# Value matmuls grouped by the height of their chunks, and a reordered list of work, in an attention and MoE kernel on one core

## Chip, cores and metric

One core of a Trainium2 chip runs the kernel. The metric is the device time of one launch in microseconds. TensorE is called PE here, its weight loads PEld, VectorE DVE, ScalarE ACT, GpSimd POOL and SyncE SP; SP issues nearly all transfers.

## What is computed

Attention over 4 batches, 8 heads, 576 positions of 64 numbers, with a bias that a small network makes of the relative position, and behind it two dense layers with h - tanh(h) between them, on 2304 tokens:

```python
scores = scale * np.matmul(q, k.transpose(0, 1, 3, 2))
x = (psi_rel / psi_i)[..., None]
bias = np.maximum(x @ w1 + b1, 0.0) @ w2
attn = softmax(scores + bias.transpose(2, 0, 1)[None, :, :, :])
x = np.matmul(attn, v)          # heads side by side: 2304 x 512
h = x @ w_in                    # 512 x 2048
out = (h - np.tanh(h)) @ w_out  # 2048 x 512
```

The inputs are fp32. The kernel splits each operand of the large matmuls into a high and a low half (hi, lo) and sums three or four products of halves.

## The kernel before

The work is written as a list of operations with the tiles that they read and write, an engine or several to choose from, an estimated duration and a priority. `Plan.order` (L158) walks through estimated time and gives each free engine the ready operation with the lowest priority number for which buffers are free. The outcome is a fixed list for each engine; on the chip each engine runs its own list in order and waits where a semaphore is not yet set. So durations in the plan issue nothing, they only set the order; SP's transfers are such a list too. `claimed` (L110) keeps shared buffers for a blocked operation of higher priority.

The operations, by the names that rows and text use:

- **pb** (`bias_group`, L417): 36 groups. Four rows hg are made on ACT, DVE or POOL (L429 to L433), PE multiplies them by w2 (L441), ACT or DVE scale the result (bo) and SP writes it to bias_d in DRAM.
- **ws, win, wout** (`weight_chunk`, L459): 32 chunks of the two weight matrices, 16 of each. A chunk is loaded into a stage buffer and split with six instructions on DVE, ACT or POOL (L469 to L488).
- **kv, qq** (L502, L513): keys with values, and queries, loaded and split.
- **ps, s, mx** (`attn_tile`, L536): scores of 128 queries by 576 keys for two heads on PE (16 matmuls, L555); DVE adds the bias and takes row minima (L569), ACT the exponential (L583), DVE the reciprocal, ACT the high half hl and DVE the low half (L599), SP the transpose of hl to pt (L609). The two PSUM tiles ps have one buffer each, so the next scores or pb wait until DVE has read the last.
- **px, xt** (`attn_values`, L617): the values. For two batches (bb) and a pair of heads (j) PE sums attention times values over 576 keys. A pair of heads has nine stored chunks of 128 rows: four for each head (i from 0 to 3), and one that both share, 64 rows each (i = 4). Each chunk is taken three times (hi by hi, hi by lo, lo by hi), so a px has 2 x 5 x 3 x 2 = 60 matmuls. The matmuls of j = 0 and 1 write to PSUM partitions 0 to 63 and 64 to 127. Before, each batch is a sum of its own, first its four chunks of 128 rows, then the shared one. ACT and DVE turn px into xt (L645, L648).
- **ph, tt, gh, gl, po** (`moe`, L656): the dense layers of a block of 128 or 256 tokens: hidden matmuls ph (L669), tanh on ACT, subtraction on DVE, halves gh and gl, output matmuls po (L696), in steps of 24 or 48.

Names carry their place: px{block}_{pair}; s{g}_{t}_{pair}_{bb}, with g a pair of batches, t a tile of 128 queries and t = 4 the half tile of 64; `BLOCKS` (L39) takes (0, 4) first. In an engine's order the scores' two tiles of s0_1_0_1 are ps0_0_1_0_1 and ps1_0_1_0_1, and a running number stands at the end.

Priorities are steps of the attention tiles plus or minus leads (L765 to L773); the weight chunks have the one line `W_P` for both matrices, taken in turn by fours. `WEIGHT` (L754) scales durations where an operation may choose its engine.

Of the kernel before, what the change touches and what calls it, by code (L numbers as in the profile page):

```python
# [300 lines left out]
def kernel(  # L301
# [157 lines left out]
    def weight_chunk(src, hi, lo, key, prio):  # L459
        st = new_stage(f"ws_{key[0]}{key[1]}_{key[2]}")  # L460
# [5 lines left out]
        move(P * 4096, lambda: st()[:, :1024].bitcast(U64), src, w=[(st, 0), (st, 1)], prio=prio)  # L466
# [69 lines left out]
    def attn_tile(g, t, p, bb, qq, bt, prio):  # L536

        half = t == HALF
        nm = f"{g}_{t}_{p}_{bb}"
# [24 lines left out]
        op("pe", c_mm(HS, 1, 2 * len(terms)), scores, r=rd, w=pss + [(s, "x") for s in rows], prio=prio)  # L564
        for j in range(2):
# [14 lines left out]
            op("dve", c_psum(S) + 80, bias_min, r=[ps, (bt, 0), (bt, 1)], w=[s, (m, j)], prio=prio, psum=True)  # L580
# [6 lines left out]
            op("act", c_act(S, 1) + 190, expo, r=[(m, j)], w=[s, (m, 2 + j)], prio=prio)  # L587
# [5 lines left out]
        op("dve", 331, recip, r=[(m, 2), (m, 3)], w=[(m, 6)], prio=prio)  # L593
        for j in range(2):
# [9 lines left out]
            op(high, r=[s, (m, 6)], w=[(hl, j, 0)], prio=prio)  # L604
            op("dve", c_dve2(S, 1), low, r=[s, (m, 6), (hl, j, 0)], w=[(hl, j, 1)], prio=prio)
# [11 lines left out]
    def attn_values(g, t, p, pts, px, xt, prio):  # L617
# [3 lines left out]
        runs = [(l, y, i) for i in range(5) for l, y in ((0, 0), (0, 1), (1, 0))]  # L621

        def mms():
            for bb in range(2):
                kw, pt, col = kvt[2 * g + bb, p], pts[0 if half else bb], 64 * bb if half else 0
                for si, (l, y, i) in enumerate(runs):
                    for j in range(2):
# [216 lines left out]
```

## Time and profile before

| | |
|---|---|
| median of 3 runs | 704.25 us (704.04 to 706.08) |
| the profiled execution | 701.42 us, of which the span from first to last instruction 699.6 us |
| TensorE's granted clock, mean | 0.945 of full speed |
| busy: PE, DVE, ACT, POOL | 630.5, 478.8, 429.0, 68.1 us |

Busy is the union of an engine's instructions; PE's ends are modelled, so a busy PE is one that always has a matmul under way. Where an engine's list waits, the profile names the instruction that ended the wait. A clock of 1.00 is 2.4 GHz, of 0.50 it is 1.2.

### The profile page before, as it was taken

The numbers are of one execution on the slowest core, as the hardware profiler recorded it, in microseconds if no ns is written. First come the engines' busy times: TensorE is split into PE (matmuls) and PEld (weight loads), VectorE is DVE, ScalarE is ACT, GpSimd is POOL, SyncE is SP. The second block draws the span as 40 slices with busy tenths as digits, with TensorE's granted clock in tenths as the row PEclk, the third lists the DMA queues.
The fourth block names the chain that finished last, engine by engine and source line by source line (L and its number), as shares of the span: only waits on it lengthen the run. The fifth ranks groups of instructions, "written<-read, shape, count | busy, mean of one in ns | idle before, by whom it ended". The sixth has DMA issues, their size and how long they took to land.

```text
span 699.6 us, 18910 instructions
## 1 busy us (share of the span) xinstructions
PE 630.5 (90%) x8096; PEld 488.0 (70%) x8096; DVE 478.8 (68%) x980; ACT 429.0 (61%) x788; POOL 68.1 (10%) x61
## 2 busy tenths in 40 slices
PE   4556566796999999999999999999999999999997
PEld 1112234684677777788888878887887888888897
DVE  5998998889866667585888867665776746532231
ACT  5768876658776767567666676666665646422221
POOL 1100111101210301100221010021000000000000
PEclk9768857899899999999999999999999999999999
DMA  7877799988775866666979876777769666630000
GB/s 251 286 275 247 235 236 309 229 180 172 191 174 96 210 151 152 110 161 139 259 200 212 187 179 137 155 149 165 152 147 154 123 124 129 119 54 31 2 31 17
DMA packets 193780, 114.25 MB, mean 163 GB/s; under 512 B 171152, under 2 KB 176416, under 8 KB 193696
## 3 DMA queue, kind: packets, MB, share of 16 engines
q1 hardware_dynamic: 193632, 113.03, 68.4%
q8 instruction: 63, 1.03, 0.6%
q14 instruction: 21, 0.17, 0.1%
q0 software_dynamic: 64, 0.02, 0.0%
HBM read 55.22 MB, written 15.34 MB: 101 GB/s over the span
## 4 chain that ended last, share of the span: by engine, by line
PE 78%; DVE 4%; ACT 1%; issue 1%; DVEq 0%; ACTq 0%
PE ph L669 28%; PE po L696 27%; PE px L630 10%; PE ps L555 10%; PE pb L441 3%; DVE s L569 1%; DVE hl L599 1%; DVE hg L431 0%; ACT hl L370 0%; DVE tt L686 0%; DVE gl L389 0%; ACT hg L429 0%; DVE win_lo L389 0%; ACT tt L681 0%; DVE bo L451 0%
## 5 line engine op out<-in xcount | busy, mean ns | idle before, releaser
L669 PE MATMUL ph<-xt,win_hi 128*128 128x256 f16 (+1 forms) x1280 | 194.5, 263 | 0.1
L669 PE MATMUL ph<-xt,win_lo 128*128 128x256 f16 (+1 forms) x640 | 162.1, 263 | 0.0
L696 PE MATMUL po<-gh,wout_h 128*128 128x256 bf16 (+1 forms) x640 | 161.9, 263 | 0.0
L696 PE MATMUL po<-gl,wout_h 128*128 128x256 f16 (+1 forms) x640 | 161.4, 262 | 0.1
L696 PE MATMUL po<-gh,wout_l 128*128 128x256 bf16 (+1 forms) x640 | 161.4, 262 | 0.0
L583 ACT ACTIVATE s<-s,mx 128x576 f32<-128x576 f32 x144 | 110.6, 769 | 55.3 <-DVE mx L569 49.1
L669 PEld LDWEIGHTS <-win_hi 128*128 128x128 f16 x1280 | 117.2, 98 | 23.0 <-issue 11.7
L696 PEld LDWEIGHTS <-wout_h 128*128 128x128 f16 x1280 | 116.5, 98 | 19.4 <-issue 7.8
L599 DVE SCALAR_TENSOR_TENSOR hl<-s,mx,hl 128x576 f16<-128x576 f32 x144 | 117.5, 847 | 9.9 <-ACT hl L370 9.6
L569 DVE CUSTOM_DVE_ANT_0 s<-ps,bt 128x576 f32<-128x576 f32 x144 | 104.7, 751 | 26.5 <-PE ps L555 26.3
L441 PE MATMUL pb<-hg,w2s 128*32 128x288 f32 x576 | 74.9, 496 | 46.1 <-ACT hg L429 19.3
L370 ACT ACTIVATE hl<-s,mx 128x576 f16<-128x576 f32 x144 | 104.3, 765 | 9.6 <-issue 6.1
L686 DVE SCALAR_TENSOR_TENSOR tt<-tt,ph 128x512 f32<-128x512 f32 x72 | 49.4, 686 | 83.3 <-ACT tt L681 83.0
L555 PE MATMUL ps<-kv,qq 64*128 64x288 f16 (+1 forms) x1280 | 90.3, 298 | 16.5 <-DVE mx L569 10.2
L681 ACT ACTIVATE tt<-ph 128x512 f32<-128x512 f32 x72 | 43.0, 597 | 99.4 <-PE ph L669 99.0
L630 PE MATMUL px<-pt,kv 128*64 128x128 f16 (+3 forms) x2400 | 85.4, 221 | 2.5 <-DMA pt<-hl 2.5
L555 PEld LDWEIGHTS <-qq 64*128 64x128 f16 (+1 forms) x1280 | 55.8, 101 | 44.8 <-issue 31.2
L441 PEld LDWEIGHTS pb<-hg,w2s 128*32 128x32 f32 x576 | 24.7, 123 | 87.3 <-ACT hg L429 40.7
L630 PEld LDWEIGHTS <-kv 128*64 128x64 f16 (+1 forms) x2400 | 69.6, 113 | 21.3 <-issue 10.6
L669 PEld LDWEIGHTS <-win_lo 128*128 128x128 f16 x640 | 62.9, 98 | 5.9
L696 PEld LDWEIGHTS <-wout_l 128*128 128x128 f16 x640 | 62.6, 98 | 6.1 <-issue 0.2
L429 ACT ACTIVATE hg<-zt,b1l 128x576 f32<-128x576 f32 x86 | 61.8, 766 | 0.0
(52 smaller groups left out, 467.5 us busy)
## 6 DMA issues: line engine op xcount, KB each, us to landing
bt<-bias_d SPq DMA_DIRECT2D x32, 576.0 KB, 4.6
bias_d<-bo SPq DMA_DIRECT2D x36, 288.0 KB, 3.6
kvst<-kv SPq DMA_DIRECT2D x16, 576.0 KB, 5.6
ws_wi<-w_in SPq DMA_DIRECT2D x16, 512.0 KB, 5.3
ws_wo<-w_out SPq DMA_DIRECT2D x16, 512.0 KB, 4.8
bt<-bias_d SPq DMA_DIRECT2D x16, 288.0 KB, 5.3
qst<-qF SPq DMA_DIRECT2D x8, 512.0 KB, 4.0
outT<-ot SPq DMA_DIRECT2D x16, 256.0 KB, 2.5
```

The source lines that it names most:

```text
L370: "act": ("act", c_act(n, ptr), lambda: A.activation(out(), in_(), AF.Copy, scale=scale() if ptr else scale)),
L429: lambda hg=hg, src=src, bs=bs: A.activation(hg(), src, AF.Relu, bias=bs, scale=1.0)),
L441: nc.tensor.matmul(pb()[32 * j : 32 * j + 32, x, :HS], w2s, hgs[j]()[:, x * HS : x * HS + HS], start=True, stop=True, tile_position=(0, 32 ...
L555: nc.tensor.matmul(pss[j]()[w * e : w * e + w, x, :HS], qq()[dp, a, c0 + w * e : c0 + w * e + w], ks()[dp, y, x * HS : x * HS + HS], start ...
L569: V.tensor_tensor_reduce(s().rearrange("p (x k) -> p x k", x=2), ps()[:, :, :HS], bt()[:, j].rearrange("p (x k) -> p x k", x=2), -0.125 / ...
L583: A.activation(s(), s(), AF.Exp, bias=m()[:, j : j + 1], scale=-1.0, accum_out=m()[:, 2 + j : 3 + j])
L599: V.scalar_tensor_tensor(hl()[:, 1, hs], s(), m()[:, 6 + j : 7 + j], hl()[:, 0, hs], ALU.mult, ALU.subtract)
L630: nc.tensor.matmul(px()[64 * j : 64 * j + 64, w * bb : w * bb + w], kw()[r, y, S + 64 * c : S + 64 * c + 64], pt()[r, NCH * l + c, col : c ...
L669: nc.tensor.matmul(ph()[:, n * (f - f0) : n * (f - f0) + n], w[:, k, f * P : f * P + P], xs[k]()[:, a, :n], start=(k == 0 and e == 0), sto ...
L681: "act", c_actp(512), lambda ph=ph, tt=tt: A.activation(tt(), ph(), AF.Tanh, scale=1.0 / SH),
L686: lambda ph=ph, tt=tt: V.scalar_tensor_tensor(tt(), tt(), -SH, ph(), ALU.mult, ALU.add),
L696: nc.tensor.matmul(po()[:, d // 2, n * (d % 2) : n * (d % 2) + n], wout[w][:, f, d * P : d * P + P], x()[:, n * (f - f0) : n * (f - f0) + ...
```

## The change

Two things. First, `attn_values` runs all chunks of 128 rows of both batches and then the shared chunks of both, with one start flag on the first matmul and one stop flag on the last. The number and shape of the matmuls are the same.

Second, the list of work. The planner's durations of scores and values are larger; weight chunks have a line of priorities for each matrix and their loads a later one (`W_LEAD`); a table `ADJ` adds to the priorities of single operations; ACT counts for less where an engine is chosen; some leads differ; `claimed` goes through the ready operations in order of priority. `DRAIN` is 0, so the five priorities with it stay.

```diff
@@ claimed
-        for o in {o for ops in cand.values() for o in ops if o.ready <= now}:
-            new = [b for b in o.bufs if not b.live]
-            if new and not self.fits(o, free, limit) and self.fits(o, free, limit, False):
-                for b in new:
-                    if b.tag in self.mixed:
-                        g = self.group[b.tag]
-                        claims[g] = min(claims.get(g, (9e9, 0)), (o.prio, o.idx))
+        ready = {o for ops in cand.values() for o in ops if o.ready <= now}
+        for o in sorted(ready, key=lambda o: (o.prio, o.idx)):
+            groups = {self.group[b.tag] for b in o.bufs if not b.live and b.tag in self.mixed}
+            if groups <= claims.keys():
+                continue
+            if not self.fits(o, free, limit) and self.fits(o, free, limit, False):
+                for g in groups:
+                    claims.setdefault(g, (o.prio, o.idx))
@@ bias_group, and likewise weight_chunk, prep_kv, prep_q, load_bias, attn_tile
+        prio += adj(f"b{t}")
@@ weight_chunk
-        move(P * 4096, lambda: st()[:, :1024].bitcast(U64), src, w=[(st, 0), (st, 1)], prio=prio)
+        move(P * 4096, lambda: st()[:, :1024].bitcast(U64), src, w=[(st, 0), (st, 1)], prio=prio - W_LEAD)
@@ attn_tile
-        op("pe", c_mm(HS, 1, 2 * len(terms)), scores, r=rd, w=pss + [(s, "x") for s in rows], prio=prio)
+        op("pe", c_mm(HS, 1, 2 * len(terms)) + 190.0, scores, r=rd, w=pss + [(s, "x") for s in rows], prio=prio)
@@ attn_values
-        runs = [(l, y, i) for i in range(5) for l, y in ((0, 0), (0, 1), (1, 0))]
+        runs = [(bb, i) for bb in range(2) for i in range(4)] + [(0, 4), (1, 4)]
 
         def mms():
-            for bb in range(2):
+            for n, (bb, i) in enumerate(runs):
                 kw, pt, col = kvt[2 * g + bb, p], pts[0 if half else bb], 64 * bb if half else 0
-                for si, (l, y, i) in enumerate(runs):
+                for m, (l, y) in enumerate(((0, 0), (0, 1), (1, 0))):
...
-                            start=(si == 0),
-                            stop=(si == len(runs) - 1),
+                            start=(n == 0 and m == 0),
+                            stop=(n == 9 and m == 2),
...
-        op("pe", 2 * len(runs) * max(c_mm(w), 53.0), mms, r=rd, w=[px, (xt, "x")], prio=prio)
+        op("pe", 3 * len(runs) * max(c_mm(w), 53.0) + 280.0, mms, r=rd, w=[px, (xt, "x")], prio=prio)
@@ the list of weight chunks
-                    win_chunk(k, c, W_P[0] + W_P[1] * (8 * c + k))
+                    win_chunk(k, c, WI_P[0] + WI_P[1] * (4 * c + k))
                 for f in range(4):
-                    wout_chunk(4 * c + f, W_P[0] + W_P[1] * (8 * c + 4 + f))
+                    wout_chunk(4 * c + f, WO_P[0] + WO_P[1] * (4 * c + f))
@@ numbers
-WEIGHT = {"swdge": 0.8, "dve": 1.125, "act": 0.931, "pool": 0.768}
+WEIGHT = {"swdge": 0.8, "dve": 1.125, "act": 0.803, "pool": 0.768}
...
-W_P = (-15.256, 0.924)
+WI_P = (-15.256, 1.848)
+WO_P = (-11.56, 1.848)
+W_LEAD = -2.426
+DRAIN = 0.0
...
```

What it moves shows in the engines' lists. In the lists of PE below one row stands for each operation, its first matmul. The first place is PE's list at the start of attention, in the half block, where scores of four pairs and the first values stand. Before:

```order
L555 MATMUL ps0_0_4_1_0_652<-kv0_1_94,qq0_4_554 64x288
...
L441 MATMUL pb11_701<-hg44_574,w2s_75 32x288
...
L555 MATMUL ps0_0_4_2_0_737<-kv0_2_144,qq0_4_554 64x288
...
L441 MATMUL pb12_798<-hg48_772,w2s_75 32x288
...
L555 MATMUL ps0_0_4_3_0_812<-kv0_3_175,qq0_4_554 64x288
...
L630 MATMUL px0_0_858<-pt0_4_0_0_726,kv0_0_88 64x64
...
L630 MATMUL px0_1_944<-pt0_4_1_0_793,kv0_1_94 64x64
```

After the change:

```order
L565 MATMUL ps0_0_4_1_0_583<-kv0_1_94,qq0_4_487 64x288
...
L446 MATMUL pb9_644<-hg36_503,w2s_75 32x288
...
L565 MATMUL ps0_0_4_2_0_666<-kv0_2_144,qq0_4_487 64x288
...
L641 MATMUL px0_0_723<-pt0_4_0_0_641,kv0_0_88 64x64
...
L446 MATMUL pb10_790<-hg40_656,w2s_75 32x288
...
L565 MATMUL ps0_0_4_3_0_816<-kv0_3_174,qq0_4_487 64x288
...
L641 MATMUL px0_1_872<-pt0_4_1_0_711,kv0_1_94 64x64
```

The first values now stand ahead of the last scores of the half block, and two bias groups fewer stand ahead of them.

The second place is PE's list in block 2, from the scores of pair 0, second batch (s0_1_0_1), to those of pair 1, second batch (s0_1_1_1). Before:

```order
L555 MATMUL ps0_0_1_0_1_2201<-kv1_0_91,qq0_1_852 128x288
...
L630 MATMUL px1_3_2233<-pt0_0_3_0_2113,kv0_3_175 64x128
...
L441 MATMUL pb19_2304<-hg76_2220,w2s_75 32x288
...
L669 MATMUL ph1_0_2322<-xt0_0_0_1644,win_hi_71 128x256
...
L555 MATMUL ps0_0_1_1_0_2361<-kv0_1_94,qq0_1_852 128x288
...
L696 MATMUL po0_1498<-gh0_12_1950,wout_h_78 128x128
...
L441 MATMUL pb20_2445<-hg80_2348,w2s_75 32x288
...
L669 MATMUL ph1_2_2458<-xt0_0_0_1644,win_hi_71 128x256
...
L555 MATMUL ps0_0_1_1_1_2499<-kv1_1_97,qq0_1_852 128x288
```

After the change:

```order
L565 MATMUL ps0_0_1_0_1_2136<-kv1_0_91,qq0_1_1030 128x288
...
L680 MATMUL ph0_12_2160<-xt0_4_0_803,win_hi_71 128x128
...
L446 MATMUL pb19_2223<-hg76_2154,w2s_75 32x288
...
L641 MATMUL px1_3_2244<-pt0_0_3_0_1932,kv0_3_174 64x128
...
L680 MATMUL ph1_0_2329<-xt0_0_0_1566,win_hi_71 128x256
...
L565 MATMUL ps0_0_1_1_0_2362<-kv0_1_94,qq0_1_1030 128x288
...
L680 MATMUL ph1_2_2384<-xt0_0_0_1566,win_hi_71 128x256
...
L446 MATMUL pb20_2421<-hg80_2307,w2s_75 32x288
...
L565 MATMUL ps0_0_1_1_1_2441<-kv1_1_97,qq0_1_1030 128x288
```

48 hidden matmuls of block 0 (ph0_12) have come behind the first scores, px1_3 behind pb19, and 48 output matmuls (po0) have left this stretch; they now stand right behind its end.

The third place is DVE's list between the minima of pairs 2 and 3 of the half block (ISA rows are the minima and their read). Before:

```order
L469 TENSOR_SCALAR ws_wo9_0_649<-ws_wo9_0_649 128x512
L469 TENSOR_SCALAR ws_wo10_0_693<-ws_wo10_0_693 128x512
L474 SCALAR_TENSOR_TENSOR ws_wo9_0_649<-ws_wo9_0_649 128x512
L590 TENSOR_SCALAR mx0_4_2_0_778<-mx0_4_2_0_778 128x2
L591 RECIPROCAL mx0_4_2_0_778<-mx0_4_2_0_778 128x2
L373 TENSOR_SCALAR ws_wo9_0_649<-ws_wo9_0_649 128x512
L474 SCALAR_TENSOR_TENSOR ws_wo10_0_693<-ws_wo10_0_693 128x512
L482 SCALAR_TENSOR_TENSOR ws_wo9_0_649<-ws_wo9_0_649 128x512
L373 TENSOR_SCALAR ws_wo10_0_693<-ws_wo10_0_693 128x512
L482 SCALAR_TENSOR_TENSOR ws_wo10_0_693<-ws_wo10_0_693 128x512
L389 TENSOR_TENSOR wout_l_79<-ws_wo9_0_649,wout_h_78 128x512
L569 ISA s0_4_3_0_0_855,mx0_4_3_0_856<-ps0_0_4_3_0_812,bt0_4_3_710 128x576
```

After the change:

```order
L579 ISA s0_4_2_0_0_786,mx0_4_2_0_787<-ps0_0_4_2_0_666,bt0_4_2_617 128x576
L579 ISA mx0_4_2_0_787 128x1
L488 SCALAR_TENSOR_TENSOR ws_wo8_0_577<-ws_wo8_0_577 128x512
L579 ISA s0_4_2_0_1_800,mx0_4_2_0_787<-ps1_0_4_2_0_668,bt0_4_2_617 128x576
L579 ISA mx0_4_2_0_787 128x1
L659 SCALAR_TENSOR_TENSOR xt0_4_0_803<-px0_0_723,xt0_4_0_803 128x128
L475 TENSOR_SCALAR ws_wi2_2_637<-ws_wi2_2_637 128x512
L436 TENSOR_SCALAR hg44_850<-zt_80,b1l_76 128x576
L600 TENSOR_SCALAR mx0_4_2_0_787<-mx0_4_2_0_787 128x2
L601 RECIPROCAL mx0_4_2_0_787<-mx0_4_2_0_787 128x2
L480 SCALAR_TENSOR_TENSOR ws_wi2_2_637<-ws_wi2_2_637 128x512
L579 ISA s0_4_3_0_0_863,mx0_4_3_0_864<-ps0_0_4_3_0_816,bt0_4_3_702 128x576
```

Weight chunks have left this stretch, and the low half of the first values (xt0_4_0, which waits for px0_0) has come into it, ahead of the minimum of pair 3.

## Rows read from the trace of the kernel before

**Rows 1.** The page, part 2: PE's busy tenths in 40 slices of 17.5 us
```profile
PE   4556566796999999999999999999999999999997
```

**Rows 2.** By stretch: us; busy us of PE, PEld, DVE, ACT, POOL; clock; DMA share, GB/s
```profile
20.00:176.00 156.00, 104.43 (x1338) 60.47 (x1338) 141.26 (x283) 114.79 (x198) 17.92 (x16) 0.78 0.88 240
176.00:183.00 7.00, 5.78 (x54) 3.26 (x56) 6.54 (x14) 5.78 (x10) 1.04 (x2) 0.51 0.76 211
183.00:630.00 447.00, 447.00 (x5829) 360.30 (x5826) 300.99 (x643) 280.28 (x540) 44.68 (x36) 1.00 0.72 154
sum 700.00, PE 630.47 PEld 488.01 DVE 478.77 ACT 429.02 POOL 68.06; mean PE 126.09 PEld 97.60 DVE 95.75 ACT 85.80 POOL 13.61
```

**Rows 3.** Waits of PE, whole span: us in total, times, longest us
```profile
PE pb L441 <- ACT hg L429: 19.3, 12, 3.8
PE ps L555 <- DVE mx L569: 10.2, 6, 4.2
PE px L630 <- DMA pt<-hl: 2.5, 1, 2.5
```

**Rows 4.** PE's timeline and chain around its last wait: start us, us
```profile
179.35 2.10 PE L555 MATMUL ps<-kv,qq 64*128 64x288 f16 x16 [0.83 <-ACT bo L450]
181.38 2.93 PE L630 MATMUL px<-pt,kv 128*64 128x128 f16 x60
...
189.24 2.79 PE po L696 x48
```

**Rows 5.** PE's timeline in narrow windows through one group px
```profile
303.05 0.86 PE L630 MATMUL px<-pt,kv 128*64 128x128 f16 x24
303.84 0.24 PE L630 MATMUL px<-pt,kv 64*64 64x128 f16 x2
304.13 0.25 PE L630 MATMUL px<-pt,kv 128*64 128x128 f16 x2
304.92 0.35 PE L630 MATMUL px<-pt,kv 64*64 64x128 f16 x6
305.21 1.15 PE L555 MATMUL ps<-kv,qq 64*128 64x288 f16 x16
```

**Rows 6.** The chain that ended last: start us, us, line and count
```profile
195.85 1.09 PE ps L555 x16
...
199.67 2.15 PE px L630 x60
201.82 1.11 PE pb L441 x16
202.93 2.73 PE ph L669 x24
...
623.60 4.25 PE px L630 x180
```

**Rows 7.** Groups of DVE instructions, shapes apart: busy us, mean ns of one
```profile
L389 DVE TENSOR_TENSOR gl<-tt,gh 128x512 f16<-128x512 f32 x50 | 35.0, 701 | 14.7 <-ACT gh L370 14.6
L431 DVE TENSOR_SCALAR hg<-zt,b1l 128x576 f32<-128x576 f32 x58 | 30.6, 556 | 0.3 <-POOL b1l L415 0.3
L389 DVE TENSOR_TENSOR win_lo<-ws_wi,win_hi 128x512 f16<-128x512 f32 x14 | 9.6, 685 | 0.2 <-ACT win_hi L370 0.2
L451 DVE TENSOR_SCALAR bo<-pb,rls 128x576 f32<-128x576 f32 x11 | 9.0, 817 | 9.5 <-PE pb L441 9.3
L389 DVE TENSOR_TENSOR qq<-qst,qq 128x1024 f16<-128x1024 f32 x3 | 4.2, 1395 | 0.0
L373 DVE TENSOR_SCALAR win_hi<-ws_wi 128x512 f16<-128x512 f32 x5 | 2.1, 420 | 0.0
```

**Rows 8.** The tile pt: its transposes
```profile
DMA to landing us min/median/max: 4.5/5.0/10.1
```

**Rows 9.** Timelines of PE and SP: the first scores, the first transpose
```profile
82.41 0.69 PE L555 MATMUL ps<-kv,qq 64*64 64x288 f16 x16 [1.04 <-ACT bo L450]
92.22 5.40 SPq L609 DMA_TRANSPOSE pt<-hl  x1
```

More of the change, by code (lines that the diff above doesn't have):

```diff
@@ L415, with adj @@
     op("pool", c_pool(144, 1), lambda: G.tensor_scalar(b1l, b1l, b1s, 1.0, ALU.mult, ALU.mult), r=["b1"], w=["b1l"], prio=-1000)
+    def adj(name):
+        return ADJ.get(name, 0.0)
     def bias_group(t, prio):
+        prio += adj(f"b{t}")
         hgs = [new_hg(f"hg{4 * t + j}") for j in range(4)]
@@ L459, in weight_chunk @@
     def weight_chunk(src, hi, lo, key, prio):
+        prio += adj("%s%d%d" % key)
         st = new_stage(f"ws_{key[0]}{key[1]}_{key[2]}")
@@ L502, in prep_kv @@
     def prep_kv(b, p, prio):
+        prio += adj(f"kv{b}{p}")
         kw, st = new_kv(f"kv{b}_{p}"), new_stage(f"kvst{b}_{p}")
@@ L513, in prep_q @@
     def prep_q(g, t, prio):
+        prio += adj(f"q{g}{t}")
         n = 512 if t == HALF else 1024
@@ L524, in load_bias @@
     def load_bias(g, t, p, prio):
+        prio += adj(f"bt{g}{t}{p}")
         bt = new_bt(f"bt{g}_{t}_{p}")
@@ L538, in attn_tile @@
         half = t == HALF
+        prio += adj(f"u{g}{t}{p}{bb}")
         nm = f"{g}_{t}_{p}_{bb}"
@@ L578, in bias_min @@
                 )
-            op("dve", c_psum(S) + 80, bias_min, r=[ps, (bt, 0), (bt, 1)], w=[s, (m, j)], prio=prio, psum=True)
+            op("dve", c_psum(S) + 80, bias_min, r=[ps, (bt, 0), (bt, 1)], w=[s, (m, j)], prio=prio - DRAIN, psum=True)
             def expo(s=s, j=j):
@@ L585, in expo @@
                 )
-            op("act", c_act(S, 1) + 190, expo, r=[(m, j)], w=[s, (m, 2 + j)], prio=prio)
+            op("act", c_act(S, 1) + 190, expo, r=[(m, j)], w=[s, (m, 2 + j)], prio=prio - 2 * DRAIN)
         def recip():
@@ L591, in recip @@
             V.reciprocal(m()[:, 6:8], m()[:, 4:6])
-        op("dve", 331, recip, r=[(m, 2), (m, 3)], w=[(m, 6)], prio=prio)
+        op("dve", 331, recip, r=[(m, 2), (m, 3)], w=[(m, 6)], prio=prio - 3 * DRAIN)
         for j in range(2):
@@ L603, in attn_tile @@
             high = narrow(S, lambda hs=hs: hl()[:, 0, hs], s, lambda j=j: m()[:, 6 + j : 7 + j], 1, kind="hi")
-            op(high, r=[s, (m, 6)], w=[(hl, j, 0)], prio=prio)
-            op("dve", c_dve2(S, 1), low, r=[s, (m, 6), (hl, j, 0)], w=[(hl, j, 1)], prio=prio)
+            op(high, r=[s, (m, 6)], w=[(hl, j, 0)], prio=prio - 3 * DRAIN)
+            op("dve", c_dve2(S, 1), low, r=[s, (m, 6), (hl, j, 0)], w=[(hl, j, 1)], prio=prio - 3 * DRAIN)
         pt = new_pt(f"pt{nm}")
@@ L766 @@
 TR_LEAD = 654.549
-KV0_LEAD = 55.926
-KV_LEAD = 1.3
-Q_LEAD = 97.336
+KV0_LEAD = 51.88
+KV_LEAD = 3.864
+Q_LEAD = 137.041
 Q0_LEAD = -2.194
@@ L772 @@
 BIAS_P = (-20, 1.684)
-W_P = (-15.256, 0.924)
+WI_P = (-15.256, 1.848)
+WO_P = (-11.56, 1.848)
+W_LEAD = -2.426
+DRAIN = 0.0
+ADJ = {"wo60": 0.437, "wo00": -0.35, "wo130": 0.423, "wi21": 0.211, "wi33": 0.41, "wi00": -0.347, "wo110": 2.613, "wo80": -1.771, "kv31": 1.833, "kv23": 0.652, "kv32": 3.471, "kv12": -1.698, "q11": -8.554, "q10": 1.355, "q12": -0.365, "q14": 0.264, "wo140": -1.074, "b31": -2.52, "kv21": -6.337, "kv13": 9.655, "u1321": -0.833, "u1231": 0.062, "b22": 0.708, "bt141": -0.039, "b15": -0.872, "bt030": -8.756}
 def _tables():
```

## The prediction

> **What bounds the kernel now.** I read first the page's slices of PE's busy time: four to seven tenths in the first eight and in the tenth, nine or more from the eleventh (175 us on) to the last but one [rows 1]. The table by stretch says what the other engines do there [rows 2]: from 183 to 630 us PE is busy for 447.00 of 447.00 us at the full clock, DVE for 301 and ACT for 280. From 20 to 176 us it is the other way round: DVE is busy for 141 of 156 us and PE for 104. The list of waits says whom PE waits for: among others the rows hg of a bias group, 19.3 us by ACT's, and DVE's row minima, which free the scores' PSUM, 10.2 us; for a transposed tile it waits once, 2.5 us [rows 3]. The last wait before the tail is 0.83 us ahead of the scores at 179.35 us [rows 4]. So there are two stages. Up to about 180 us the instructions of DVE set the pace; from there on the end is that moment plus the work left on PE. The last 70 us, with 4 us of waits behind the last hidden and output matmuls, hold no values and keep their order.
>
> **The value matmuls.** A group px has 60 matmuls in 30 pairs; the two of a pair go to the two column halves of the array. In the kernel before, a group runs 12 pairs over chunks of 128 keys, 3 pairs on the shared chunk of 64, and the same again for the second batch. The timeline of one group [rows 5] shows what each turn costs: the first long run starts at 303.05, the short one at 303.84, the next long one at 304.13, the short one at 304.92, and the scores behind it at 305.21. Twelve pairs and a turn take 0.79 us, three pairs and a turn 0.29 (303.84 to 304.13). The difference, 0.50 us for 9 pairs, is 0.0556 us a pair. A whole group takes 2.15 us on the chain [rows 6]; 30 pairs are 1.67 of it, so the four turns are 0.48, 0.12 each. After the change a group has 24 long pairs, then 6 short ones: two turns fewer, **0.24 us**, 11% of a group. The number of matmuls stays 60.
>
> The Trainium skill ("TensorEngine Tiling (Array Packing)", Key Properties) says that a change of tiling mode drains the engine, and the trace agrees that a turn costs, by 0.12 us. "TensorE: Matmul & The Clock Gate" (Step-by-step) gives some 128 cycles for a drain; an estimate by it alone, 128 cycles at 2.4 GHz, would be 0.05 us a turn and 3.4 us for the whole gain; no row here shows a turn that cheap, and I go by the measured 0.12.
>
> How many of them count? Of the 40 groups, px0_0 to px1_2 run ahead of the last wait, where PE stands still anyway: nothing. px1_3 runs at 181.38 us [rows 4], on the border of the two stages; I leave it out. The 32 groups of px2 to px9 run in the stretch in which PE never stops: 32 x 0.24 = **7.7 us**. For the four groups of px9 (64 columns, three of them in 4.25 us [rows 6]) the price of a turn is taken over from the wide ones; at nothing for these four the sum is 6.7. Turns between operations don't change it: counted in the two orders, PE goes from one kind of operation to another (hidden and output matmuls as one kind) 212 times in both.
>
> **The order of the start.** The lists differ most here. DVE's list ahead of the first minimum of pair 0 of the half block (s0_4_0) has 103 rows in place of 121; ahead of s0_1_0_1 296 in place of 307; ahead of s0_1_1_0 318 in place of 321. So attention is pulled ahead of weight chunks, which come later, and by s0_1_1_0 both lists have done nearly the same. I price that last place by kinds [rows 7]: on L373 six more win_hi and one more wout_h, four fewer ws_wi and two fewer ws_wo, all of one shape, net one at 0.42; two more qq of 1024 columns (1.395); one win_lo less (0.685) and one ws_wo of L482 less, taken at the same price; five hg fewer (0.556); one bo more (0.817): 0.42 + 2.79 - 0.69 - 0.69 - 2.78 + 0.82 = **-0.1 us**. And PE, in its list, has by then done the same set of operations in both kernels (the second place in the lists above). If DVE keeps its pace, this place comes at the same time, and behind it lies 7.7 us less work: the sum is **-7.8 us**.
>
> One place further the picture is less kind. In the order before, 48 output matmuls of block 0 (po0, 2.79 us at 189.24 [rows 4]) stand between s0_1_1_0 and s0_1_1_1; now they come behind it. If DVE still bounds there, the gain is 7.7 - 2.8 + 0.1 = 5.0 us. But in the trace PE no longer waits there, and DVE does not fill its time (from 183 us on it is busy for 67%), so I take this as the low end only. One place earlier it is kinder: ahead of s0_1_0_1 DVE has 11 instructions fewer, at its mean of 478.77 us / 980 = 0.49 us some 5.4 us [rows 2], while 48 hidden matmuls (ph0_12, 2.79 us as the same shape elsewhere takes [rows 4]) are pushed behind it. If nothing waits after that, the gain is 7.7 + 5.4 - 2.8 = 10.3 us.
>
> **What costs nothing by this reading.** Other choices of engine: 11 of the subtractions gl go from POOL to DVE, 11 x 0.701 = 7.7 us [rows 7]; they lie nearly all behind 183 us, where DVE has 146 us to spare [rows 2]; without that cover they would eat the gain. Matmul costs in the planner (190 and 280 ns more), DRAIN (0) and the claims of buffers issue nothing; they act through the order alone. Scores and values stand closer in PE's list: summed with the durations of [rows 6], 17.5 us of work at the least lay between a pair's last scores and its px, and 31 in the mean (px2 to px8); now it is 15.9 and 24, and 1.1 for the scores themselves. A transpose needs 4.5 to 10.1 us to land [rows 8], and the chain ahead of it some 10 (scores at 82.41, transpose issued at 92.22 [rows 9]). So 14.5 to 20 us are needed and 17 are there: at most 3 us each, at the two or three closest places; I take zero, since the median landing is 5.0.
>
> **The rivals.**
> *The start gains too.* The place that decides moves to s0_1_0_1 as worked out: -10.3; and the slow stretch of 176 to 183 us (clock 0.51, the lower of the two levels, behind a stretch in which PE had gaps in a third of the time [rows 2]) can fall into waiting time, which gives back half of the 3.6 us behind 179.35, so 1.8 more: -12.1, 692.2 us. For it: attention starts earlier by 18 DVE instructions. Against: DVE is at 91% already (141 of 156), and its total ahead of s0_1_1_0 is unchanged.
> *The turns do not go away,* because what costs is not the shape but the change of weights or of the sum: then only -0.1 is left, 704.1. Against: the long runs also change weights with each pair, at 0.056 us, without such a gap.
> *DVE waits in its own queue: slower.* DVE now has the second half of xt0_4_0 queued ahead of the minimum s0_4_3 (third place), and PE has px0_0 ahead of pb10 and of the scores of pair 3. px0_0 waits for a transpose; behind it on PE wait pb10 and the scores, and on DVE all that is queued behind xt, weight chunks too. In a stage that DVE bounds each such wait goes to the end. The place is the eight groups px0 and px1; the one wait of this kind in the trace is 2.5 us [rows 3]. From 7.8 / 8 = 0.98 us each it eats the whole gain; at 2.5 us in five of eight the time is 12.5 - 7.8 = 4.7 us longer, 709.0. Against: DVE's list holds 38 instructions between s0_4_0 and that xt, 18.6 us at the mean of 0.49, and 14.5 to 20 us plus px (2.15 us [rows 6]) are needed, so 0 to 3.4 us are missing at that place; the seven others I take to be no worse.
>
> **How the numbers follow.** The profiled execution took 701.42 us, 699.6 of it the span; the median of the runs is 704.25, 0.4% above. I take the difference from the median: 704.25 - 7.8 = **696.5 us** (the profiled execution itself would come to 693.6). Chances: the forecast with its low end (-5.0 to -9) 0.61; the start gains too 0.18; the turns stay, or the start loses what the turns give 0.11; slower by waits on DVE 0.10. A measurement tells about 0.3%, 2.1 us, from no change: faster 0.79 (the first two), same 0.11, slower 0.10. The range goes from the second case, 691.5, to just inside no change, 702.8; about 0.2 is left out.
>
> **What would show it.** In the profile after, a px group on the chain should take 1.91 us in place of 2.15, in two runs of 48 and 12 matmuls, and PE's busy time should fall by some 9 us. PE's last wait should lie at 180 to 197 us, ahead of the scores of block 2's pairs 0 or 1 (s0_1_0 and s0_1_1). If px keeps 2.15 us the turns were not the cause. If PE's waits for px or the scores grow ahead of 183 us, the third rival is at work, and DVE's busy share between 20 and 180 us will have dropped. Waits of px on transposes behind 200 us would show that scores and values stand too close.

## The result, and the profile after

| | before | after |
|---|---|---|
| median on the same chip | 704.14 us (4 runs) | 692.42 us (691.25 to 693.11, 4 runs) |
| ratio after to before | | 0.9826, 95% interval 0.9804 to 0.9848 |
| the profiled execution, its span | 701.42, 699.6 us | 691.25, 689.5 us |
| busy: PE, DVE, ACT, POOL | 630.5, 478.8, 429.0, 68.1 us | 620.9, 481.3, 433.5, 52.8 us |

The change is worth 11.7 us in the medians and 10.1 us between the two profiled spans. The forecast was 696.5 (691.5 to 702.8): the time is in the range, 4.1 us below the forecast and 0.9 us above the lower end.

The page of the kernel after, its parts 1 and 2 (slices of 17.2 us; PEclk is the granted clock in tenths):

```profile
PE 620.9 (90%) x8096; PEld 487.2 (71%) x8096; DVE 481.3 (70%) x983; ACT 433.5 (63%) x795; POOL 52.8 (8%) x51
...
PE   4566557957999999999999999999999999999997
...
PEclk9658555996999999999999999999999999999999
```

The picture of [rows 1] is still there: gaps in the first ten slices, none behind. PE is busy 9.6 us less, nearly all of the gain, and idle for 68.6 us in place of 69.1. The table by stretch of the kernel after (us; busy us of PE, PEld, DVE, ACT, POOL; clock; DMA share, GB/s):

```profile
20.00:176.00 156.00, 104.56 (x1329) 61.64 (x1322) 140.08 (x282) 116.53 (x201) 18.03 (x18) 0.72 0.90 246
176.00:183.00 7.00, 6.42 (x124) 5.00 (x122) 6.93 (x18) 6.41 (x14) 2.67 (x3) 1.00 1.05 187
183.00:630.00 447.00, 445.86 (x5905) 365.24 (x5905) 307.52 (x648) 285.64 (x547) 28.84 (x24) 1.00 0.72 153
```

Against [rows 2], DVE is as busy as before up to 176 us, POOL gives work to DVE behind 183 us, and the stretch from 176 to 183 us runs at the full clock (2.4 GHz) where it ran at 0.51. From 20 to 176 us, where PE waits for DVE, the granted clock is lower than before, 0.72 against 0.78. Next, the kernel after's chain of waits (start us, us, line and count): a group px, one run of three groups of px9, and 48 output matmuls of block 0.

```profile
191.62 2.79 PE po L707 x48
194.41 1.91 PE px L641 x60
...
614.12 3.55 PE px L641 x180
```

A group takes 1.91 us in place of the 2.15 of [rows 6]; three groups of px9 take 3.55 in place of 4.25, 0.23 less each. The 48 output matmuls now run behind the scores of s0_1_1_1. Those are the last row of PE's timeline in the kernel after; the first row is s0_1_0_1, the third s0_1_1_0:

```profile
174.09 1.16 PE L565 MATMUL ps<-kv,qq 64*128 64x288 f16 x16 [0.83 <-ACT bo L455]
...
183.00 0.27 PE L680 MATMUL ph<-xt,win_hi 128*128 128x256 f16 x1 [0.52 <-DVE xt L659]
...
184.62 1.15 PE L565 MATMUL ps<-kv,qq 64*128 64x288 f16 x16
...
190.46 1.16 PE L565 MATMUL ps<-kv,qq 64*128 64x288 f16 x16 [0.86 <-ACT bo L455]
```

The last wait of more than 0.3 us before the tail is 0.86 us at 190.46 us, ahead of s0_1_1_1; before it was at 179.35, ahead of s0_1_0_1 [rows 4]. The list of PE's waits of the kernel after (us in total, times, longest us), to be held against [rows 3]:

```profile
PE pb L446 <- ACT hg L434: 18.3, 13, 3.2
...
PE ps L565 <- DVE mx L579: 7.0, 4, 4.3
...
PE px L641 <- DMA pt<-hl: 0.8, 1, 0.8
```

PE waits once for a transposed tile, for 0.8 us. The wait that the third rival was built on did not come.

### The profile page after: what moved, and what is told of

Read it like the earlier page. It is cut to its first block, busy times and chain, and to the rows that moved or that the text cites. A ratio compares the mean times of both kernels' runs of the same rounds, so it can differ in the third digit from the quotient of the medians.

```text
span 689.5 us, 18880 instructions
## 1 busy us (share of the span) xinstructions
PE 620.9 (90%) x8096; PEld 487.2 (71%) x8096; DVE 481.3 (70%) x983; ACT 433.5 (63%) x795; POOL 52.8 (8%) x51
## 4 chain that ended last, share of the span: by engine, by line
PE 82%; DVE 8%; ACT 4%; DMA 3%; issue 2%; POOL 0%; SPq 0%; ACTq 0%; DVEq 0%; POOLq 0%
PE ph L680 28%; PE po L707 27%; PE ps L565 11%; PE px L641 9%; PE pb L446 7%; DVE hl L609 2%; DVE s L579 2%; DMA ws_wi<-w_in 1%; ACT hg L434 1%; ACT bo L455 1%; DMA kvst<-kv 1%; DMA w1s<-w1c 1%; DMA ws_wo<-w_out 1%; DVE kv L515 1%; DVE ws_wi L488 0%
## 5 line engine op out<-in xcount | busy, mean ns | idle before, releaser
L680 PEld LDWEIGHTS <-win_hi 128*128 128x128 f16 x1280 | 117.6, 99 | 21.7 <-issue 10.2
L707 PEld LDWEIGHTS <-wout_h 128*128 128x128 f16 x1280 | 116.8, 98 | 21.7 <-issue 10.6
L609 DVE SCALAR_TENSOR_TENSOR hl<-s,mx,hl 128x576 f16<-128x576 f32 x144 | 119.8, 860 | 8.1 <-ACT hl L371 8.1
L446 PE MATMUL pb<-hg,w2s 128*32 128x288 f32 x576 | 72.3, 514 | 46.0 <-ACT hg L434 18.3
L371 ACT ACTIVATE hl<-s,mx 128x576 f16<-128x576 f32 x144 | 104.8, 765 | 12.1 <-issue 4.5
L641 PE MATMUL px<-pt,kv 128*64 128x128 f16 (+3 forms) x2400 | 76.2, 220 | 0.8 <-DMA pt<-hl 0.8
L641 PEld LDWEIGHTS <-kv 128*64 128x64 f16 (+1 forms) x2400 | 67.1, 114 | 13.6 <-issue 9.9
L434 ACT ACTIVATE hg<-zt,b1l 128x576 f32<-128x576 f32 x96 | 68.7, 763 | 0.0
```

Source lines behind the costliest of these rows:

```text
L371: "act": ("act", c_act(n, ptr), lambda: A.activation(out(), in_(), AF.Copy, scale=scale() if ptr else scale)),
L434: lambda hg=hg, src=src, bs=bs: A.activation(hg(), src, AF.Relu, bias=bs, scale=1.0)),
L446: nc.tensor.matmul(pb()[32 * j : 32 * j + 32, x, :HS], w2s, hgs[j]()[:, x * HS : x * HS + HS], start=True, stop=True, tile_position=(0, 32 ...
L609: V.scalar_tensor_tensor(hl()[:, 1, hs], s(), m()[:, 6 + j : 7 + j], hl()[:, 0, hs], ALU.mult, ALU.subtract)
L641: nc.tensor.matmul(px()[64 * j : 64 * j + 64, w * bb : w * bb + w], kw()[r, y, S + 64 * c : S + 64 * c + 64], pt()[r, NCH * l + c, col : c ...
L680: nc.tensor.matmul(ph()[:, n * (f - f0) : n * (f - f0) + n], w[:, k, f * P : f * P + P], xs[k]()[:, a, :n], start=(k == 0 and e == 0), sto ...
```

## Experiments

Two theories stand against each other. The first is that of the forecast: the turns of px give 7.7 us, and the start of the list gives nothing. The second is the first rival: the start gains as well. The runs are compared with the kernel before on the same chip, whose medians were 704.14, 703.51, 703.89 and 704.02 us in the four sets.

### The new values alone, in the old order

The loops and flags are those of the change, in the kernel before:

```diff
@@ attn_values
-        runs = [(l, y, i) for i in range(5) for l, y in ((0, 0), (0, 1), (1, 0))]
+        runs = [(bb, i) for bb in range(2) for i in range(4)] + [(0, 4), (1, 4)]
...
-                            start=(si == 0),
-                            stop=(si == len(runs) - 1),
+                            start=(n == 0 and m == 0),
+                            stop=(n == 9 and m == 2),
```

> The order of the values' chunks alone, every engine's list of operations as before. Theory: each px loses two turns, 0.24 us, and from the last wait at 179 us on PE never stops, so 32 groups give 7.7 us: 696.4 us, px at 1.91 us, last wait of PE unmoved at 179.35 us. The rest of the measured gain of 11.7 us, 4.0, is then the list's. Rival: PE's shorter values open waits elsewhere behind 180 us and less than 5 us arrive. Second rival: the early groups count as well, 40 x 0.24 = 9.6 us, 694.5.

Measured: 694.57 us (694.05 to 697.25), ratio 0.9883 (0.9847 to 0.9919), span 692.9. From its chain and from PE's timeline (the scores of s0_1_0_1, the bias group behind px1_3, the scores of s0_1_1_0 and s0_1_1_1):

```profile
217.43 1.91 PE px L630 x60
```

```profile
180.59 1.16 PE L555 MATMUL ps<-kv,qq 64*128 64x288 f16 x16 [0.83 <-ACT bo L450]
...
184.80 1.18 PE L441 MATMUL pb<-hg,w2s 128*32 128x288 f32 x16 [1.11 <-DVE mx L569]
...
188.63 1.16 PE L555 MATMUL ps<-kv,qq 64*128 64x288 f16 x16
...
196.34 1.16 PE L555 MATMUL ps<-kv,qq 64*128 64x288 f16 x16
```

The kernel before starts s0_1_1_0 and s0_1_1_1 at 188.08 and 195.79 us; here they start no earlier. The gain of 6.7 us in the span is that of px behind them. One part of the expectation failed: PE's last wait did not stay at 179.35 us. With the shorter px1_3 PE waits another 1.11 us for DVE's minima, at 184.80 us. The median, 694.57, is also what the second rival named (all 40 groups count). The two starts speak against it, as far as one execution can: the early groups brought nothing forward.

### The new order alone, with the old values

The reverse, in the kernel after:

```diff
@@ attn_values
-        runs = [(bb, i) for bb in range(2) for i in range(4)] + [(0, 4), (1, 4)]
+        runs = [(l, y, i) for i in range(5) for l, y in ((0, 0), (0, 1), (1, 0))]
...
-                            start=(n == 0 and m == 0),
-                            stop=(n == 9 and m == 2),
+                            start=(si == 0),
+                            stop=(si == len(runs) - 1),
```

> The list of work of the change alone; inside a px the chunks run as before, with four turns. Theory: the two parts add up, so this gives the 4.0 us that the values leave: 700.1 us, px at 2.15 us, PE's last wait earlier than 195 us ahead of s0_1_1_1, and no slow clock between 176 and 183 us. Rival: the list gains nothing by itself (704), since it was made for shorter values, and the gain of both needs both. Second rival: the list carries most of it (694 or less).

Measured: 698.16 us (697.0 to 699.26), ratio 0.9924 (0.9897 to 0.995), span 696.1. From its chain and PE's timeline (s0_1_1_0 and s0_1_1_1):

```profile
211.13 2.15 PE px L641 x60
```

```profile
183.90 1.15 PE L565 MATMUL ps<-kv,qq 64*128 64x288 f16 x16
...
189.75 1.16 PE L565 MATMUL ps<-kv,qq 64*128 64x288 f16 x16 [0.86 <-ACT bo L455]
```

The list alone gains 3.5 us of span and 5.4 us in the medians, with px at its old price; by the interval of the ratio it is 3.5 to 7.3 us. So the forecast's -0.1 for the start was wrong. In the spans the two parts add up: 6.7 + 3.5 = 10.2, and both together gave 10.1. In the medians they come to 8.9 + 5.4 = 14.3 against 11.7; by the ratios and their intervals the parts are 8.2 (give or take 2.5) and 5.4 (2.0), and both together 12.3 (1.6). So they add up within some 3 us, and the closer fit of the spans is in part luck.

### Is it the turn? More of them, and none

In the kernel before, every product goes through the long chunks and then the shared one:

```diff
@@ attn_values
-        runs = [(l, y, i) for i in range(5) for l, y in ((0, 0), (0, 1), (1, 0))]
+        runs = [(l, y, i) for l, y in ((0, 0), (0, 1), (1, 0)) for i in range(5)]
```

> Before's list; in each px the shared chunk comes once for each of the three products, so a batch turns six times and a px twelve times in place of four. Theory, the turn costs 0.12 us: 8 x 0.12 = 0.96 us more for a px (3.1 us), 32 groups in the busy stretch: 30.7 us more, 735 us. Rival, the cost lies in the start and end of a sum, of which there are as many as before: 704 us, px at 2.15.

And in the kernel before, the shared chunk goes over all 128 rows, so that its part of the values is another sum, with as many matmuls:

```diff
@@ attn_values
-                        r = slice(64 * j, 64 * j + 64) if i == 4 else slice(0, P)
+                        r = slice(0, P)
```

> Before's list and order of chunks, but the shared chunk is taken over all 128 rows for both heads, which makes its part of the values another sum; the matmuls are then all of one shape, with the same chunks, weights and sums. Theory, the change of shape costs: no turns but the one into px and the one out, px at 1.67 to 1.9 us; 0.36 to 0.48 us less for 32 groups, 11.5 to 15.4 us: 689 to 693 us. Rival, the change of chunk, of weights or of the sum costs: 704 us, px at 2.15.

Measured, one run each: 735.86 us and 692.06 us. A px on the chain of the first and of the second:

```profile
202.30 3.10 PE px L630 x60
```

```profile
200.82 1.79 PE px L630 x60
```

With the same 60 matmuls a px takes 1.79 us without a change of shape inside, 1.91 with one (after), 2.15 with three (before) and 3.10 with eleven: 0.12 us for each, whichever pair of kernels is taken. The turn to the next operation stands in all four.

### Or the sum? One sum with the old order of chunks

```diff
@@ attn_values
-                            start=(si == 0),
-                            stop=(si == len(runs) - 1),
+                            start=(bb == 0 and si == 0),
+                            stop=(bb == 1 and si == len(runs) - 1),
```

> The kernel before with one edit: a px is one group of sums, with one start flag and one stop flag, and its chunks keep the old order (long, short, long, short). If the change of shape is what costs, a px keeps its 2.15 us and the profiled execution stays at 701 to 702 us. If what costs is the start of a new sum in the middle of a group, a px falls towards 1.92 us and the time towards 695 us.

Measured, one run: 704.9 us, span 703.1. Its chain, and its scores of s0_1_1_1 on PE's timeline:

```profile
220.57 2.15 PE px L630 x60
```

```profile
199.24 1.15 PE L555 MATMUL ps<-kv,qq 64*128 64x288 f16 x16
```

A px keeps its 2.15 us, so the flags of the sums cost nothing; the change of shape does. The span is 3.5 us longer than before's 699.6, and all of that lies ahead of s0_1_1_1, which starts at 199.24 in place of 195.79. From there to the end it is 503.9 us, before 503.8. The list is the same in both, so this is how much one list's start moves from one execution to the next. DVE is as busy up to the first minimum of s0_1_1_0 in both (164.9 us); what differs is its idle time there, 28.8 us in place of 25.3. More on that below.

### What DVE's work is worth, early and late

In the kernel after, DVE issues the same instruction twice; the lists stay as they are. The first kernel does so in `weight_chunk`, the second in `moe`:

```diff
@@ minus
+        def on_dve():
+            for _ in range(times):
+                V.tensor_tensor(out(), a(), b(), ALU.subtract)
...
-            ("dve", c_dve2(n), lambda: V.tensor_tensor(out(), a(), b(), ALU.subtract)),
+            ("dve", c_dve2(n), on_dve),
@@ weight_chunk
-        op(minus(512, lo, lambda: words(1), hi), r=[(st, 1), key + ("h",)], w=[key + ("l",)], prio=prio)
+        op(minus(512, lo, lambda: words(1), hi, 2 if key[0] == "wi" else 1), r=[(st, 1), key + ("h",)], w=[key + ("l",)], prio=prio)
@@ moe
-            op(minus(512, gl, tt, gh), r=[tt, gh], w=[gl], prio=top)
+            op(minus(512, gl, tt, gh, 2 if 2 <= i <= 6 else 1), r=[tt, gh], w=[gl], prio=top)
```

> The kernel after with the same order, in which DVE makes the low half of each of its 13 chunks of w_in (win_lo) twice; all 13 lie ahead of the scores of s0_1_1_0. That is 13 x 0.685 = 8.9 us more work for DVE in the first stage; the result is unchanged. If DVE's work ahead of the last wait sets when that wait ends, the end comes up to 8.9 us later, 699 to 701.5 us. If DVE's idle time in that stage (some 23 us) takes it up, the time stays at 692 to 693 us.

> The kernel after with the same order, in which DVE makes the low half gl twice in blocks 2 to 6, 33 times, all behind 190 us. That is 33 x 0.70 = 23 us more work for DVE in the second stage; the result is unchanged. If PE alone sets the pace there, the time stays at 692 to 693 us, as the forecast took it for the gl that came over from POOL. If DVE counts there too, it goes towards 715 us.

Measured: early 698.36 us (697.12 to 700.16), ratio 0.9926 (0.9902 to 0.995), span 696.5; late 694.48 us (691.86 to 695.09), ratio 0.9861 (0.9833 to 0.9889), span 692.9. The doubled group of the first kernel and that of the second (busy us, mean ns of one):

```profile
L390 DVE TENSOR_TENSOR win_lo<-ws_wi,win_hi 128x512 f16<-128x512 f32 x26 | 17.8, 689 | 0.8 <-ACT win_hi L371 0.3
```

```profile
L390 DVE TENSOR_TENSOR gl<-tt,gh 128x512 f16<-128x512 f32 x94 | 66.2, 705 | 18.5 <-ACT gh L371 17.0
```

In the first, s0_1_1_1 starts at

```profile
197.18 1.16 PE L569 MATMUL ps<-kv,qq 64*128 64x288 f16 x16 [0.86 <-ACT bo L459]
```

that is 6.7 us later than in the kernel after, for 9.0 us of work (13 x 0.689). So two thirds to three quarters of what DVE does more in the first stage reaches the end (5.9 us in the medians, 7.0 between the spans). The rest falls into its idle time: up to the first minimum of s0_1_1_0 that is 21.7 us in place of 24.2. In the second, 33 more gl, 23 us of work, cost 2.1 us in the medians, with overlapping intervals; and half of the 3.4 us between the spans lies ahead of the first doubled instruction, since s0_1_1_1 starts there at 192.17 in place of 190.46. The list of PE's waits from 183 to 630 us in the second kernel:

```profile
PE ps L569 <- DVE mx L583: 1.5, 1, 1.5
...
PE ph L684 <- DVE xt L663: 0.5, 1, 0.5
```

PE waits there for 1.5 us in one place. A microsecond of DVE costs about 0.7 ahead of 183 us and less than 0.1 behind it: the two stages of the forecast are shown, and with them that gl from POOL to DVE costs next to nothing (by this price 11 of them, 7.7 us, would cost 0.7).

### Which part of the list?

Four kernels take one part of the list back, from the kernel after. First the table of single priorities and the planner's durations:

```diff
@@ first kernel
+ADJ = {}
@@ second kernel
-        op("pe", c_mm(HS, 1, 2 * len(terms)) + 190.0, scores, r=rd, w=pss + [(s, "x") for s in rows], prio=prio)
+        op("pe", c_mm(HS, 1, 2 * len(terms)), scores, r=rd, w=pss + [(s, "x") for s in rows], prio=prio)
...
-        op("pe", 3 * len(runs) * max(c_mm(w), 53.0) + 280.0, mms, r=rd, w=[px, (xt, "x")], prio=prio)
+        op("pe", 3 * len(runs) * max(c_mm(w), 53.0), mms, r=rd, w=[px, (xt, "x")], prio=prio)
```

> The kernel after without its table of single priorities (ADJ empty); all other numbers stay. By my sum over its list (work of DVE ahead of the last waiting scores, with the durations of the profile after, plus the work left on PE) the end comes 4 to 6 us earlier than in the kernel after, 687 to 689 us. If the gain at the start was earned by that table, it goes with it: 3.5 to 5 us later than after, 696 to 697.5 us. A px takes 1.92 us by both.

> The kernel after with the planner's old durations of scores and values (without the added 190 and 280 ns); all other numbers stay, the matmuls too. By my sum over its list the end comes about 1 us earlier than in the kernel after, 691 to 692 us: same. If the truer durations earned the gain at the start, it is 3.5 to 5 us later, 696 to 697.5 us.

Then the weights' line of priorities, and the leads:

```diff
@@ third kernel
-                    win_chunk(k, c, WI_P[0] + WI_P[1] * (4 * c + k))
+                    win_chunk(k, c, WI_P[0] + WI_P[1] * (8 * c + k))
-                    wout_chunk(4 * c + f, WO_P[0] + WO_P[1] * (4 * c + f))
+                    wout_chunk(4 * c + f, WI_P[0] + WI_P[1] * (8 * c + 4 + f))
-WI_P = (-15.256, 1.848)
+WI_P = (-15.256, 0.924)
-W_LEAD = -2.426
+W_LEAD = 0.0
@@ fourth kernel
-WEIGHT = {"swdge": 0.8, "dve": 1.125, "act": 0.803, "pool": 0.768}
+WEIGHT = {"swdge": 0.8, "dve": 1.125, "act": 0.931, "pool": 0.768}
-KV0_LEAD = 51.88
-KV_LEAD = 3.864
-Q_LEAD = 137.041
+KV0_LEAD = 55.926
+KV_LEAD = 1.3
+Q_LEAD = 97.336
```

> The kernel after with the one old line of priorities for the weight chunks of both matrices and their loads not set later (W_LEAD 0). By my sum over its list 1 to 2 us earlier than after, 690.5 to 691.5 us: same. If the later weight chunks earned the gain at the start (less work of DVE ahead of the scores of s0_1_1_0), it is 3.5 to 5 us later, 696 to 697.5 us.

> The kernel after with four numbers of the kernel before: KV0_LEAD, KV_LEAD, Q_LEAD and the weight of ACT. DVE's list has 316 rows ahead of the first minimum of s0_1_1_0, where after has 319 and before 322, so by DVE's work the time is that of after within 1.5 us, 691 to 694 us. If these leads earned the gain at the start, it is 3.5 to 5 us later, 696 to 697.5 us.

| taken back | median, us | ratio to before, 95% interval | span |
|---|---|---|---|
| table ADJ | 722.04 (718.55 to 725.02) | 1.0276 (1.0235 to 1.0317) | 716.8 |
| durations | 693.19 (692.96 to 694.65) | 0.9856 (0.983 to 0.9882) | 691.2 |
| weights' line | 692.08 (691.17 to 693.19) | 0.9837 (0.9809 to 0.9864) | 689.2 |
| leads, weight of ACT | 694.36 (692.38 to 694.77) | 0.9861 (0.9836 to 0.9886) | 692.9 |

Three of the four leave the time within 2 us of the kernel after, and their intervals overlap with its own: none of these parts alone earns more than that. Without the table both expectations were far off. The table by stretch of that kernel (columns as above):

```profile
183.00:227.00 44.00, 43.88 (x467) 39.35 (x466) 14.54 (x24) 11.78 (x20) 0.00 (x0) 1.00 0.10 19
227.00:280.00 53.00, 36.74 (x434) 21.22 (x432) 35.64 (x82) 35.38 (x67) 3.17 (x2) 0.71 0.75 171
```

and waits of SP's queue from 170 to 240 us and of DVE from 192 to 227 us:

```profile
SPq L400 <- ACT ot L381: 43.1, 2, 38.2
```

```profile
DVE tt L697 <- ACT tt L692: 21.0, 6, 5.2
```

From 192 to 227 us this list holds nothing but dense layers on PE. PE is full, but DVE stands in its queue behind ph and tt, busy for a third of the time, SP stands for 38 us behind the store of one ot, and nothing of attention is made. When the dense work is used up, PE has gaps again for 53 us, busy 37 of them, at a mean clock of 0.71. My sum had put this kernel at 687 to 689 us because it counted DVE's work ahead of the scores and PE's work left; DVE's waiting stands in neither.

The third kernel says something else. Its first scores come 12 us later than in the kernel after. In PE's timeline, first its scores of the half block, then those of the kernel after:

```profile
84.32 1.50 PE L565 MATMUL ps<-kv,qq 64*64 64x288 f16 x31 [0.63 <-ACT bo L455]
```

```profile
71.69 1.41 PE L565 MATMUL ps<-kv,qq 64*64 64x288 f16 x32 [1.41 <-ACT qq L371]
```

and yet its s0_1_1_1 starts at 188.87 us, no later than after's 190.46. (Ahead of that place it has 48 output matmuls more, 24 hidden ones and 16 of a bias group fewer, about 1 us less in sum.) So the earlier start of attention is not what gains.

## Why the prediction held, and what was mis-sized

**The time is in the range, but not by the forecast's sum.** The turn and the stages held; the start, put at nothing, gave several microseconds. The range holds 692.42 because its lower end was set at the case of the first rival.

**The stages** are as said: one paced by DVE, then PE alone. Doubled instructions of DVE cost about 0.7 of their time in the first and less than 0.1 in the second.

**The turn**, 0.12 us, two fewer in a px, is right at four counts of turns, and it is the shape and not the sum. The Trainium skill ("TensorE: Matmul & The Clock Gate", Step-by-step) gives some 128 cycles for the drain of a matmul, 0.05 us as an estimate at 2.4 GHz; the runs decide for 0.12, at the full clock. Taking the price over for px9 was right too: 0.23 us each.

**How many count** can be read by splitting each span at the start of s0_1_1_1 on PE, behind the last wait of after. Behind that place PE hardly waits until the tail (0.3 us in the kernel after), so the length repeats where the lists and the values are the same (503.8 and 503.9; 499.0 and 499.3), while the time up to it does not:

| kernel | list | start of s0_1_1_1 | from there to the end |
|---|---|---|---|
| before | before | 195.79 | 503.8 |
| one sum | before | 199.24 | 503.9 |
| new values alone | before | 196.34 | 496.6 |
| no turns inside | before | 196.94 | 493.4 |
| more turns | before | 198.42 | 535.7 |
| after | after | 190.46 | 499.0 |
| new order alone | after | 189.75 | 506.4 |
| gl twice | after | 192.17 | 500.7 |
| win_lo twice | after | 197.18 | 499.3 |

The px term is 496.6 - 503.8 = -7.2 in the old list and 499.0 - 506.4 = -7.4 in the new one, where the forecast had -7.7. (These and the sums below are from starts and spans of one execution each.) The 48 output matmuls that moved behind the place cost 506.4 - 503.8 = 2.6 in the old form and 2.4 in the new one; the forecast had 2.8, in its low end. Both terms hold. Three turns fewer and eight more for each of 32 groups would be -11.5 and +30.7; the other two kernels measure -10.4 and +31.9 there, so such a sum is good to some 1.2 us.

**The start is the term that was mis-sized.** The forecast put it at -0.1 us at s0_1_1_0. On PE's timeline of the kernel before, the scores of s0_1_1_0 and s0_1_1_1 stand at

```profile
188.08 1.16 PE L555 MATMUL ps<-kv,qq 64*128 64x288 f16 x16
195.79 1.15 PE L555 MATMUL ps<-kv,qq 64*128 64x288 f16 x16
```

and in the kernel after at 184.62 and 190.46: 3.5 and 5.3 us earlier. The way from the one to the other takes 7.70 to 7.71 us in all five kernels with before's list and 5.84 to 5.85 in all four with after's. The moved output matmuls make that 2.8 shorter, and a new wait takes 0.9 back: pb20 now stands right ahead of the scores, which wait 0.86 us until ACT has read it. So the change of the span splits into -3.5 at s0_1_1_0, +0.9 for that wait, -2.8 and +2.5 for the moved matmuls and -7.3 for px. That is -10.2 us, measured -10.1; since the terms are pieces of the same two spans, the agreement proves nothing, but it says where the gain lies. Up to s0_1_1_0's first minimum, at 190.2 us before and 186.6 after, the tables of one stretch have, first before, then after:

```profile
0.00:190.20 190.20, 125.00 (x1547) 72.45 (x1548) 164.87 (x321) 138.22 (x232) 25.20 (x27) 0.80 0.86 239
```

```profile
0.00:186.60 186.60, 123.08 (x1537) 73.03 (x1538) 162.36 (x319) 136.39 (x229) 25.05 (x29) 0.76 0.89 244
```

DVE is busy 2.5 us less and idle 1.1 us less (25.3 and 24.2). Two things failed in the step. First the prices by kind: means over the whole kernel [rows 7] are not the prices of the instructions that changed. I took a qq of 1024 columns at 1.395 and a hg at 0.556. In these stretches, before and then after, they are

```profile
L389 DVE TENSOR_TENSOR qq<-qst,qq 128x1024 f16<-128x1024 f32 x1 | 1.7, 1747 | 0.0
L431 DVE TENSOR_SCALAR hg<-zt,b1l 128x576 f32<-128x576 f32 x36 | 20.1, 584 | 0.3 <-POOL b1l L415 0.3
```

```profile
L390 DVE TENSOR_TENSOR qq<-qst,qq 128x1024 f16<-128x1024 f32 x3 | 3.7, 1220 | 0.3 <-ACT qq L371 0.3
L436 DVE TENSOR_SCALAR hg<-zt,b1l 128x576 f32<-128x576 f32 x31 | 15.8, 541 | 0.3 <-POOL b1l L416 0.3
```

so two more qq came to 2.0 us together, not 2.79, and five hg fewer to 4.3, not 2.78. The same groups in the kernel with the new order alone say 2.0 and 3.3, so the price of the hg is known to 1 us. With these two the kinds that differ come to some -2.4 in place of -0.1, which is nearly DVE's whole change; kinds whose counts did not move shift by up to 1.9 us (hl), but cancel. Second, waits. DVE's waits for loads of w_in up to that place, before, and the group of the same instructions in the kernel after (busy, mean, and the idle time ahead of them):

```profile
DVE ws_wi L469 <- DMA ws_wi<-w_in: 3.3, 4, 1.0
```

```profile
L475 DVE TENSOR_SCALAR ws_wi<-ws_wi 128x512 uint32<-128x512 uint32 x16 | 6.7, 420 | 0.6 <-DMA ws_wi<-w_in 0.5
```

Before, DVE waited 3.3 us for loads of w_in, after 0.5; other waits took most of that back. "If DVE keeps its pace" was the assumption that a list of work can't back.

**One profile is thin for such a term.** Five executions of before's list start s0_1_1_1 at 195.79 to 199.24 us, three of after's at 189.75 to 192.17: means of 197.35 and 190.79, 6.6 apart, with a spread of 3.5 and 2.4 us inside a list. (The five differ in px, of which 8 of 40 groups run ahead of that place; win_lo twice is left out, since it has more work there.) The difference is outside the spread, its size is known to some 2 us. With 6.6 in place of 5.3 the gain would be 11.4 us, near the 11.7 of the medians; that the two profiled executions, 10.1 apart, were simply a close pair is likely, but not shown.

**The rivals.** The first came true in its half of the start: 696.5 was off by what this rival named, and its 692.2 is 0.2 us from the median. Its working is nearer the two timelines than the forecast's, too. At s0_1_0_1, where it set the end, after is 5.3 us earlier (174.09 against 179.35), and it had 5.4; the 48 hidden matmuls behind it cost the 2.8 that it took. But its condition, that nothing waits after that, does not hold: PE waits 0.52 us for xt at 183.00 and 0.86 at 190.46, which by the starts cost 0.9 us each. So its -12.1 is 2 us too much for the spans, and that it meets the median to 0.2 us is partly luck. Its 1.8 us of clock can't be told apart from the list. The scores of s0_1_0_1 and px1_3 do take 3.0 us in after where they took 4.9 at the lower level, 0.24 of that for the turns. But the kernel with the new values alone has the old list and runs the scores at 180.59 us at the full clock (1.16 us against the 2.10 of [rows 4]), and there PE waits 1.11 us for DVE's minima instead, at 184.80: the way from s0_1_0_1 to s0_1_1_0 is only 0.7 us shorter (8.04 against 8.73). In the old list most of the slow clock fell into time that DVE set anyway. That the turns stay, and that DVE waits in its own queue, did not happen. (In the third rival 20 us and a px of 2.15 less 18.6 are 3.6 us, not 3.4; nothing hangs on it.)

**The low end** (-5.0) named s0_1_1_1, and PE does wait there last. Its reason is not borne out: it had DVE still bound that place, so that the 2.8 us would be lost. What PE waits for there is ACT's reading of pb20, so moving the matmuls cost 0.6 us in sum (-2.8, +0.9, +2.5).

**What stays open** is which numbers of the list earn the start. Durations, weights' line and leads each can go without a measurable loss; the table can't, but what its absence costs is another stall, so it is not shown that the table earns the start either. The new `claimed` and parts of the table were not tried.

## What to carry over

Where matmuls of different heights are summed, group them by height: each change of shape cost 0.12 us here, where sixty matmuls of one shape took 1.79, and there were as many matmuls as before. For a reordered list, split the span at the last wait: the part behind it could be summed here to about 1 us from counts and durations, while the part ahead needs more than one execution and must count the waits of the engine that sets the pace as well as its work, with the prices of that stretch. A list that fills one engine for long with work of one kind (35 us of dense layers in the kernel without the table) can leave the other engines idle, and their work is then missing later.

## What the runs showed that was not expected

- The start and stop flags of a sum cost nothing that shows: a px with one sum and one with two both took 2.15 us.
- The same list reached the same place up to 3.5 us apart (195.79 to 199.24 us), with DVE as busy (164.9 us) and waiting for longer, and behind it the length repeated to 0.1 us (503.8 and 503.9).
- The granted clock from 176 to 183 us differs between kernels with the same list: 0.51 before, 0.75 with one sum, 0.76 with the new values alone, 1.00 at full height. The way from s0_1_0_1 to s0_1_1_0 took 8.73, 8.66, 8.04 and 8.50 us there, which does not follow the clock.
- Scores right behind a bias group waited for ACT's reading of it by the same length each time: s0_1_0_1 for 0.83 us in all nine executions of the table, s0_1_1_1 for 0.86 in the four with after's list.
